# Narrow attention products on TensorE: taken in pairs or when overdue, instead of one by one in the order of their due times

## The chip, the cores and the metric

The kernel runs on one core of one Trainium2 chip. The metric is the device time of one execution in microseconds (us); three executions of each kernel are timed and their median is compared. One further execution is taken by the hardware profiler, and all rows of the profile come from that one.

## What is computed

A windowed attention is followed by two two-layer perceptrons, all in float32:

```python
B, H, S, D = 4, 8, 576, 64              # 2304 tokens, d_model 512, d_ff 2048
rel = pos[:, None] - pos[None, :]
mask = (0 <= rel) & (rel < 32)                          # heads 0 to 3
mask = (0 <= rel) & (rel < 128) & (rel % 4 == 0)        # heads 4 to 7
x = softmax(where(mask, q @ k.T / 8, -1e9)) @ v         # 2304 x 512
x = elu(x @ w1_in) @ w1_out
h = x @ w2_in
out = (h * clip(h + 3, 0, 6) / 6) @ w2_out
```

## The kernel before

**Precision.** Each float32 operand of a wide product is split into a high and a low part, and a product is the sum of three passes (high by high, high by low, low by high). The attention's products are single passes.

**Phase 1** (until about 467 us in the profile) is attention and the first perceptron. The tokens go in five blocks of 384, 512, 512, 512 and 384 columns. Each block goes through 16 slices of d_ff (`tile1`). For each slice, `g1` makes 12 products into PSUM tile `h` (L646), ScalarE and VectorE form the ELU and its split `ghl`, and `g2` makes 12 products into the four tiles `yp` (L702). In the first block the weights are also unpacked and split on VectorE, ScalarE and GpSimd (`convert`, `weights1`; tiles `raw` and `w`).

**Attention** goes in 18 units of 128 tokens (`unit`). Units 0 to 2 feed block 0, 3 to 6 block 1, 7 to 10 block 2, 11 to 14 block 3 and 15 to 17 block 4. The units of a block are spread over the work of the block before. A unit has three narrow products on TensorE, each written as one job:

- `scores` (L486, tile `ps`): 32 products of 64 columns; needs the loaded `q` and `k`, a PSUM bank, and a buffer `s`.
- `turn` (L536, tile `pp`): 4 transposes of 128 columns; needs the softmax of its unit. That is `low` and `top` on VectorE (L493, L502), eight `expos` on ScalarE (L521), `norm` (L527, L528) and `scale` (L531).
- `pv` (L560, tile `po`): 32 products of 64 columns; needs the two copies `turned` of `pp` into `pt`, and `v`. After it, `x_hi` and `x_lo` (L567, tile `xl`) write the block's input.

From unit 3 on, these three share the two PSUM banks of tag `a`. `q`, `k` and `v` have one buffer each, so that the next unit's `q` and `k` are loaded behind this unit's `scores`, and its `v` behind this unit's `pv` (L441, on the DMA queue of SyncE).

**The order of the work** is fixed when the program is written, by a planner (`Plan.run`). Each job has a due time `key`, a cost for each engine that it may run on, the jobs that it needs, and the buffers that it takes. For each engine the planner walks the ready jobs in order of `key`. It takes the first, unless a later one can start over 0.05 us sooner. So an engine never waits while a ready job is left, and a job early by its key fills a hole. The engines then run their queues in exactly this order. Costs and keys are the planner's own estimates.

The due times of units follow from the block starts `TB` (30.0, 107.1, 204.7, 302.3 and 397.2 by the planner's costs):

```python
unit(A1[b] // UN + u, TB[b - 1] + CFG["ATT0"] + u * (TB[b] - TB[b - 1]) * 0.93 / n, 0)
```

With `ATT0` = 3 this gives 33.0, 50.9, 68.9 and 86.8 for units 3 to 6; 110.1, 132.8, 155.5 and 178.2 for units 7 to 10; 207.7, 230.4, 253.1 and 275.7 for units 11 to 14; and 305.3, 334.7 and 364.1 for units 15 to 17. `scores` has the unit's key, `turn` 0.5 more and `pv` 0.7 more.

**Phase 2** is the second perceptron: L900 (tile `hq`) and L989 (tile `m`). The change touches none of its jobs.

Of the kernel before, what the change touches and what calls it, by code (L numbers as in the profile page):

```python
# [40 lines left out]
CFG = dict(  # L41
    T0=30.0, AT=2.6,
    AHEAD=6,
    LEAD=10.0,
    LAG=12.0,
    PREP0=40.0,
    PREP1=-25.0,
    ATT0=3.0,
    LO="P",
    ELU="A",  # L50
    BUFS=dict(g=11, e=2, y=3, ghl=3, q=1, k=1, v=1, pt=1),
    WARM=46.0,
    FROM=1.6,
    FULL=3, MPE=3, KM=5.0,
    VL=3.0,
    S2=5,
# [38 lines left out]
class Plan:  # L95
# [6 lines left out]
    def job(self, key, fn, opts, need=(), dma=0.0, takes=()):  # L102
        j = Job(key, fn, opts, need, dma)
        for ring, users in takes:
            users.append(j)
            j.takes.append((ring, users))
        self.jobs.append(j)
        return j

    def run(self):  # L110
        free = dict.fromkeys("TDAPS", 0.0)
        queue = 0.0
        pool = []
        ready = {e: [] for e in free}
        left = {}

        def enter(j):
            j.ready = max((n.end + lag + (0.25 if n.eng == "T" else 0.1) for n, lag in j.need), default=0.0)
            for e in j.opts:
                ready[e].append(j)  # L120
                ready[e].sort(key=lambda x: x.key)

        for j in self.jobs:
            left[j] = len(j.need)
            for n, _ in j.need:
                n.after.append(j)
        for j in self.jobs:
            if not left[j]:
                enter(j)
        todo = len(self.jobs)  # L130
        while todo:
            best = None
            for e, t0 in free.items():
                pick = None
                for n, j in enumerate(ready[e]):
                    if n >= 60 and pick:
                        break
                    t = max(t0, j.ready)
                    if pick and t > pick[0] - 0.05:
                        continue  # L140
                    for ring, _ in j.takes:
                        r = ring.ready(sum(x is ring for x, _ in j.takes))
                        t = 1e9 if r is None else max(t, r + 0.1)
                    if t >= 1e9 or pick and t > pick[0] - 0.05:
                        continue

                    if any(
                        max(free[o], t) + d < t + j.opts[e] + (CFG["BIAS"] if e == "D" and o == "A" else -0.02)
                        for o, d in j.opts.items() if o != e
                    ):  # L150
                        continue
                    pick = (t, j)
                if pick and (best is None or pick[0] < best[0]):
                    best = (*pick, e)
            assert best, [(e, [(x.key, x.fn) for x in r[:5]]) for e, r in ready.items()]
            t, j, e = best
            d = j.opts[e]
            if e == "T" and t < CFG["WARM"]:
                self.fill(free[e], t)
            for o in j.opts:  # L160
                ready[o].remove(j)
            for ring, users in j.takes:
                ring.take(users)
            j.eng = e
            if e == "D" and getattr(j, "sbuf", True):

                end, w = t, d
                for a, b in pool[-8:]:
                    if b > end:
                        g = max(a - end, 0.0)  # L170
                        if w <= g:
                            break
                        w -= g
                        end += g
                        z = min((b - end) * 0.42, w)
                        w -= z
                        end += z / 0.42
                d = end + w - t
            if e == "P":
                pool.append((t, t + d))  # L180
            free[e] = t + d + (0.0 if e == "T" else 0.02)
            j.end = t + d
            if j.dma:
                queue = max(queue, t + d + 1.4) + j.dma
                j.end = queue + 0.7
            j.fn(e)
            todo -= 1
            for a in j.after:
                left[a] -= 1
                if not left[a]:  # L190
                    enter(a)
# [3 lines left out]
def tile_window_attention_two_mlps(  # L195
# [228 lines left out]
    U1 = A1[1] // UN  # L424

    def unit(u, key, step):
        b = next(b for b in range(NB1) if A1[b + 1] > u * UN)
        t0 = u * UN - A1[b]
# [35 lines left out]
        while sum(w for _, w, _ in runs) < NB:  # L464
            n = sum(w for _, w, _ in runs)
            runs.append((n, next(w for w in range(NB - n, 0, -1) if len(set(masks[n:n + w])) == 1), masks[n]))

        full = u < CFG["FULL"]
        pe_masks = u < CFG["MPE"]
# [103 lines left out]
        n = NB * KW  # L573
        take1 = [(RINGS[tags[0]], bu[0])]
        if pe_masks:
            j0 = job(key - CFG["KM"], masked, {"T": 0.25}, [setup if full else setups], 0, take1)
            bu[0].append(j0)
        j1 = job(
            key, scores, {"T": 0.071 * 2 * NB}, [ld["q"], ld["k"], j0 if pe_masks else setups],
            0, [*([] if pe_masks else take1), (RINGS["s"], su), (RINGS["st"], stu)],  # L580
        )
# [18 lines left out]
        else:  # L600
# [8 lines left out]
        j6 = job(  # L609
            key + 0.5, turn, {"T": 0.12 * NB / 2}, [j5, zeros[u % len(pts)]], 0,  # L610
            [(RINGS[tags[1]], bu[1]), (RINGS[f"p{u % len(pts)}"], pu)],
        )
# [5 lines left out]
        j8 = job(key + 0.7, pv, {"T": 0.066 * 2 * NB}, [*j7, ld["v"]], 0, [(RINGS[tags[2]], bu[2])])  # L618
# [17 lines left out]
            x_users[b][z].extend([j9, j10])  # L636
        x_done.setdefault(b, []).append(j10)
        att_users.extend([j8, j10])


    PASSES = ((0, 0), (0, 1), (1, 0))
# [492 lines left out]
    def fill(t0, t1):  # L1134

        n = int((t1 - max(t0, CFG["FROM"]) - 0.35) / (0.44 if not t0 else 0.24))
        r = RINGS["h"].ready(1)
# [8 lines left out]
    with tc.manual_schedule():  # L1146
# [3 lines left out]
        for u in range(U1):  # L1150
            unit(u, CFG["ATT0"] + CFG["K0"] + u * CFG["KS"], 0)
# [3 lines left out]
        for b in range(1, NB1):  # L1155
            n = W1[b] // UN
            for u in range(n):
                unit(A1[b] // UN + u, TB[b - 1] + CFG["ATT0"] + u * (TB[b] - TB[b - 1]) * 0.93 / n, 0)
# [82 lines left out]
def program(inputs):  # L1241
    import numpy as _np
    import concourse.bacc as _bacc
    import concourse.tile as _tile
    from concourse import mybir as _mybir

    nc = _bacc.Bacc("TRN2", target_bir_lowering=False, num_devices=1, dynamic_dma_scratch_size=1024)
    arrays, args = {}, []
    for name, a in layout(**inputs).items():
        arrays[f"in_{name}_dram"] = a  # L1250
        args.append(nc.dram_tensor(f"in_{name}_dram", a.shape, _mybir.dt.from_np(a.dtype), kind="ExternalInput").ap())
    for i, (shape, dtype) in enumerate(_OUTS):
        dt = _mybir.dt.from_np(_np.dtype(dtype))
        args.append(nc.dram_tensor(f"out_{i}_dram", shape, dt, kind="ExternalOutput").ap())
    with _tile.TileContext(nc) as tc:
        tile_window_attention_two_mlps(tc, *args)
    return nc, arrays
# [8 lines left out]
```

## Time and profile before

| | before |
|---|---|
| median of 3 executions | 864.72 us (862.34 to 866.33) |
| the profiled execution | 864.24 us |
| its span, first to last instruction | 862.5 us |
| TensorE busy | 843.7 us, 98% of the span |
| VectorE, ScalarE, GpSimd busy | 64%, 47%, 14% |
| mean granted TensorE clock | 0.998 |

Units and their products are numbered in the order in which they appear in the trace. PE is TensorE, PEld its weight loads, DVE VectorE, ACT ScalarE, POOL GpSimd, SP SyncE and SPq its DMA queue.

### The profile page before, as it was taken

The page shows a single profiled execution, that of the slowest core. Times are in us where ns is not written, and L with a number is a line of the kernel's source. Part 1 is how long each engine was busy: PE and PEld are TensorE (multiplying, and loading weights), DVE is VectorE, ACT ScalarE, POOL GpSimd, SP SyncE. Part 2 cuts the span into 40 slices and gives each one's busy share as a digit, 9 for nine tenths or more (in the row PEclk, how much of TensorE's full clock was granted, in tenths as well). Part 3 has the DMA queues.
Part 4 walks back from the last instruction along what each step waited for, and adds up shares of the span by engine and source line. Part 5 has one row for each costly group of instructions (what it writes and reads, how often), then busy time and mean ns, then how long its engine had stood idle before and what let it go on. Part 6 is the DMA issues. An engine that isn't in the chain of part 4 may idle for free.

```text
span 862.5 us, 15275 instructions
## 1 busy us (share of the span) xinstructions
PE 843.7 (98%) x5692; PEld 751.1 (87%) x5692; DVE 551.5 (64%) x1156; ACT 403.5 (47%) x999; POOL 123.6 (14%) x137
## 2 busy tenths in 40 slices
PE   8899999999999999999999999999999999999996
PEld 7799988888888888888999888899999999999995
DVE  4999996766878783333343546756575657565673
ACT  3878865666747663242332434333343333333341
POOL 3565431222223300000000000100010010000000
PEclk9999999999999999999999999999999999999999
DMA  9958436877678870300764866887787878789785
GB/s 364 384 208 320 169 136 237 284 269 243 236 263 287 290 270 26 134 1 10 230 207 121 296 243 225 299 274 267 269 292 248 271 273 280 254 278 336 271 265 187
DMA packets 71273, 205.27 MB, mean 238 GB/s; under 512 B 7456, under 2 KB 25888, under 8 KB 71200
## 3 DMA queue, kind: packets, MB, share of 16 engines
q1 hardware_dynamic: 71200, 204.31, 68.4%
q8 instruction: 45, 0.74, 0.3%
q14 instruction: 28, 0.23, 0.1%
HBM read 171.77 MB, written 32.51 MB: 237 GB/s over the span
## 4 chain that ended last, share of the span: by engine, by line
PE 88%; DVE 5%; DMA 4%; ACT 2%; issue 1%; POOL 0%; SPq 0%; DVEq 0%; ACTq 0%; POOLq 0%
PE hq L900 23%; PE yp L702 20%; PE h L646 20%; PE m L989 19%; PE po L560 2%; DMA y<-x2d 2%; PE ps L486 2%; DMA wx<-w2do 1%; DVE raw L306 1%; PE pp L536 1%; DVE raw L303 1%; DVE o L1067 1%; DMA raw<-in_w_in_dram 1%; DVE w L250 1%; ACT pt L250 1%
## 5 line engine op out<-in xcount | busy, mean ns | idle before, releaser
L702 PE MATMUL yp<-ghl,w 128*128 128x512 f32 (+1 forms) x960 | 212.9, 370 | 0.0
L900 PE MATMUL hq<-x,w 128*128 128x512 f32 (+1 forms) x960 | 211.9, 370 | 0.0
L646 PE MATMUL h<-xh,w 128*128 128x512 f32 (+1 forms) x640 | 198.3, 371 | 1.9 <-DVE e L680 1.9
L702 PEld LDWEIGHTS yp<-ghl,w 128*128 128x128 f32 x960 | 173.7, 188 | 23.1
L900 PEld LDWEIGHTS hq<-x,w 128*128 128x128 f32 x960 | 164.5, 189 | 26.5
L646 PEld LDWEIGHTS h<-xh,w 128*128 128x128 f32 x640 | 118.7, 188 | 19.1 <-DVE e L680 3.5
L646 PE MATMUL h<-xl,w 128*128 128x512 f32 (+1 forms) x320 | 117.8, 368 | 0.2 <-DVE xl L567 0.2
L253 DVE TENSOR_TENSOR gz<-gf,gz 128x640 fp32r<-128x640 f32 x72 | 59.2, 823 | 81.4 <-ACT gz L250 81.4
L919 ACT ACTIVATE g<-hq 128x256 f32<-128x256 f32 x144 | 50.7, 383 | 117.3 <-PE hq L900 83.2
L250 ACT CAST gz<-gf 128x640 fp32r<-128x640 f32 x72 | 52.4, 727 | 103.2 <-PE m L989 89.0
L680 DVE SCALAR_TENSOR_TENSOR e<-e,h 128x512 f32<-128x512 f32 (+1 forms) x80 | 50.3, 628 | 76.4 <-ACT e L669 76.1
L666 ACT ACTIVATE e<-h 128x512 f32<-128x512 f32 (+1 forms) x80 | 44.3, 553 | 111.7 <-PE h L646 109.5
L989 PE MATMUL m<-w,gz 128*128 128x256 f32 x648 | 95.3, 283 | 0.0
L924 DVE SCALAR_TENSOR_TENSOR g<-g,hq 128x256 f32<-128x256 f32 x144 | 56.9, 417 | 57.2 <-ACT g L919 53.6
L989 PEld LDWEIGHTS m<-w,gz 128*128 128x128 f32 x648 | 87.4, 191 | 2.3
L646 PEld LDWEIGHTS h<-xl,w 128*128 128x128 f32 x320 | 60.1, 188 | 7.7 <-DVE xl L567 0.4
L989 PE MATMUL m<-wx,gz 128*128 128x256 f32 x432 | 63.6, 283 | 0.0
L253 POOL TENSOR_TENSOR x<-y,x 128x256 fp32r<-128x256 f32 x17 | 13.5, 812 | 328.3 <-ACT x L250 271.9
L989 PEld LDWEIGHTS m<-wx,gz 128*128 128x128 f32 x432 | 57.0, 192 | 0.0
L253 DVE TENSOR_TENSOR ghl<-e,ghl 128x512 fp32r<-128x512 f32 (+1 forms) x77 | 55.6, 722 | 2.3 <-ACT ghl L250 0.2
L306 DVE SCALAR_TENSOR_TENSOR raw<-raw 128x512 int32<-128x512 int32 x64 | 52.5, 828 | 2.3 <-ACT raw L295 0.8
L253 POOL TENSOR_TENSOR w<-raw,w 128x512 fp32r<-128x512 f32 x32 | 46.9, 1475 | 41.9 <-ACT w L250 24.6
(78 smaller groups left out, 959.6 us busy)
## 6 DMA issues: line engine op xcount, KB each, us to landing
wx<-w2do SPq DMA_DIRECT2D x72, 768.0 KB, 4.3
w<-w2di SPq DMA_DIRECT2D x80, 512.0 KB, 5.2
raw<-in_w_in_dram SPq DMA_DIRECT2D x32, 512.0 KB, 5.9
raw<-in_w_out_dram SPq DMA_DIRECT2D x32, 512.0 KB, 6.5
w2do<-stg SPq DMA_DIRECT2D x56, 256.0 KB, 2.3
q<-in_q_dram SPq DMA_DIRECT2D x18, 512.0 KB, 3.8
v<-in_v_dram SPq DMA_DIRECT2D x18, 512.0 KB, 4.0
w2di<-stg SPq DMA_DIRECT2D x32, 256.0 KB, 3.8
```

The lines of the kernel that those rows point to most:

```text
L250: (nc.scalar.copy if e == "A" else nc.vector.tensor_copy)(out=out, in_=in_)
L253: ENG[e].tensor_tensor(out=out, in0=in0, in1=in1, op=ALU.subtract)
L306: nc.vector.scalar_tensor_tensor(out=hi(), in0=hi(), scalar=3, in1=lo(), op0=ALU.logical_shift_left, op1=ALU.bitwise_or)
L486: nc.tensor.matmul(pe[c * KW:(c + 1) * KW, n, :], t["q"][:, c, n, :], kk[:, c], start=not pe_masks, stop=not pe_masks or n == NB - 1)
L646: nc.tensor.matmul(h, w[:, a, c * P:(c + 1) * P], x[b][:, c, :], start=(c == 0 and s == 0), stop=(c == KD - 1 and s == 2),)
L666: nc.scalar.activation(out=r["e"], in_=r["h"], func=AF.Relu, scale=-1.0)
L680: nc.vector.scalar_tensor_tensor(out=r["e"], in0=r["e"], scalar=-1.0, in1=r["h"], op0=ALU.add, op1=ALU.max)
L702: nc.tensor.matmul(ys[b, n], w[:, a, n * P:(n + 1) * P], g[:, c, :], start=(i == 0 and s == 0), stop=(i == KF - 1 and s == 2),)
L900: nc.tensor.matmul(r["h"], w[:, a, d * P:(d + 1) * P], x2[c, d][:, z, :], start=(d == 0 and s == 0), stop=(d == KD - 1 and s == 2),)
L919: nc.scalar.activation(out=g_t[b, j][:, k], in_=r["h"][:, h * N2:(h + 1) * N2], func=AF.Relu, bias=3.0)
L924: nc.vector.scalar_tensor_tensor(out=g_t[b, j][:, k], in0=g_t[b, j][:, k], scalar=6.0, in1=r["h"][:, h * N2:(h + 1) * N2], op0=ALU.min, op ...
L989: nc.tensor.matmul(ms[k], g, w[:, c, :], start=(j == 0 and z == 0 and s == 0), stop=(j == KP - 1 and z == len(PRODS[n]) - 1 and s == 2),)
```

## The change

For units 3 to 17 the three jobs `scores`, `turn` and `pv` (`j1`, `j6`, `j8`) are marked `short`. When the planner chooses for TensorE at its time `t0`, it looks at the short jobs whose needs are met by then (`j.ready <= t0`; whether a buffer is free is not asked). There are three cases:

1. If the job that TensorE took last was short and another short one is ready, that one goes ahead of everything else.
2. Otherwise, if exactly one short job is ready and `t0` is below its key plus `WAIT` (6 us), it is left out of the choice, also where TensorE would have nothing else to do.
3. Otherwise the order is that of before.

```diff
+    WAIT=6.0,
...
         todo = len(self.jobs)
+        last = False
         while todo:
             best = None
             for e, t0 in free.items():
                 pick = None
-                for n, j in enumerate(ready[e]):
+
+                short = [j for j in ready[e] if getattr(j, "short", False) and j.ready <= t0] if e == "T" else []
+                if last and short:
+                    order = short + [j for j in ready[e] if j not in short]
+                elif len(short) == 1 and t0 < short[0].key + CFG["WAIT"]:
+                    order = [j for j in ready[e] if j not in short]
+                else:
+                    order = ready[e]
+                for n, j in enumerate(order):
                     if n >= 60 and pick:
                         break
...
+            if e == "T":
+                last = getattr(j, "short", False)
...
+        if u >= U1:
+            for x in (j1, j6, j8):
+                x.short = True
```

## Rows read from the trace of the kernel before

**Rows 1.** Busy time by stretch: length, busy us (instructions) by engine, granted clock, DMA share, GB/s.
```profile
core 0: us, PE busy (x) PEld busy (x) DVE busy (x) ACT busy (x) POOL busy (x), PEclk, DMA share, GB/s
...
25.00:40.00 15.00, 12.45 (x128) 11.45 (x125) 14.57 (x26) 12.41 (x36) 9.90 (x7) 1.00 0.94 369
40.00:60.00 20.00, 18.87 (x186) 17.88 (x185) 19.70 (x29) 15.19 (x41) 10.28 (x8) 1.00 0.60 226
60.00:80.00 20.00, 19.46 (x163) 18.55 (x162) 19.96 (x31) 16.71 (x43) 10.52 (x7) 1.00 0.85 311
80.00:104.00 24.00, 23.82 (x212) 22.59 (x212) 23.65 (x38) 20.73 (x51) 12.90 (x9) 1.00 0.55 200
...
120.00:416.00 296.00, 296.00 (x1839) 244.09 (x1838) 187.59 (x352) 159.57 (x399) 52.87 (x57) 1.00 0.56 194
```

**Rows 2.** Chain of work that ended last, 153 to 172 us: start, us, what.
```profile
154.28 1.08 PE ps L486 x32
155.37 2.94 PE yp L702 x12
158.31 2.72 PE h L646 x12
161.03 2.72 PE yp L702 x12
163.75 0.44 PE pp L536 x4
164.19 2.77 PE h L646 x12
166.96 1.08 PE po L560 x32
168.05 2.94 PE yp L702 x12
```

**Rows 3.** The same chain where two narrow products touch, units 11, 12 and 15, 16.
```profile
218.93 0.44 PE pp L536 x4
219.37 1.08 PE ps L486 x32
220.45 2.94 PE h L646 x12
...
318.39 1.08 PE ps L486 x32
319.47 0.58 PE pp L536 x4
320.06 2.77 PE yp L702 x12
```

**Rows 4.** SP's DMA queue behind unit 9's scores: start, us, engine, line, what.
```profile
155.41 0.33 SPq L441 DMA_DIRECT2D q<-in_q_dram  x1
```

**Rows 5.** DMA issues by kind: count, KB each, median us from issue to landing.
```profile
q<-in_q_dram SPq DMA_DIRECT2D x18, 512.0 KB, 3.8
```

**Rows 6.** TensorE's timeline: scores of unit 3, unit 4; unit 5, then the rest of unit 4.
```profile
25.05 1.10 PE L486 MATMUL ps<-k,q 128*64 128x64 f32 x32
...
35.70 1.15 PE L486 MATMUL ps<-k,q 128*64 128x64 f32 x32
38.87 0.63 PE L536 MATMUL pp<-ident,s 128*128 128x128 f32 x4 [2.03 <-ACT w L250]
...
53.22 1.15 PE L486 MATMUL ps<-k,q 128*64 128x64 f32 x32
54.30 0.66 PE L536 MATMUL pp<-ident,s 128*128 128x128 f32 x4
...
58.20 1.15 PE L560 MATMUL po<-pt,v 128*64 128x64 f32 x32 [1.13 <-DVE s L493]
```

**Rows 7.** TensorE's timeline: scores of unit 6; units 5, 7; units 6, 8, 6.
```profile
63.67 1.15 PE L486 MATMUL ps<-k,q 128*64 128x64 f32 x32
...
78.19 0.60 PE L536 MATMUL pp<-ident,s 128*128 128x128 f32 x4
78.72 1.15 PE L486 MATMUL ps<-k,q 128*64 128x64 f32 x32
...
95.92 0.63 PE L536 MATMUL pp<-ident,s 128*128 128x128 f32 x4
96.48 1.15 PE L486 MATMUL ps<-k,q 128*64 128x64 f32 x32
97.81 1.15 PE L560 MATMUL po<-pt,v 128*64 128x64 f32 x32 [0.18 <-ACT pt L250]
```

**Rows 8.** VectorE's timeline: last inputs (`xl`) of block 1 and of block 3.
```profile
101.30 0.68 DVE L567 TENSOR_TENSOR xl<-po,xh 128x512 fp32r<-128x512 f32 x1
...
296.71 0.69 DVE L567 TENSOR_TENSOR xl<-po,xh 128x512 fp32r<-128x512 f32 x1
```

**Rows 9.** TensorE's timeline: block 1's first product, block 0's left-over products, block 3's first.
```profile
103.20 0.39 PE L646 MATMUL h<-xh,w 128*128 128x512 f32 x1
...
108.07 4.33 PE L702 MATMUL yp<-ghl,w 128*128 128x384 f32 x24
...
306.04 0.39 PE L646 MATMUL h<-xh,w 128*128 128x512 f32 x1
```

## The prediction

> **What bounds the kernel now.** The busy times by stretch come first, as they show where TensorE's order can matter [rows 1]. From 120 to 416 us TensorE is busy for all of its 296.00 us, at a granted clock of 1.00. There only its own work counts: whatever a narrow product costs it is paid in full, and nothing is waited for. From 25 to 104 us it is different. VectorE is busy 14.57 + 19.70 + 19.96 + 23.65 = 77.88 of 79 us, while TensorE has 12.45 + 18.87 + 19.46 + 23.82 = 74.60. In this stretch VectorE, with the unpacking of weights, sets the pace, and TensorE has 4.4 us of holes. The change adds and removes no instruction. It can act in three ways: by what it costs TensorE to go between wide and narrow products, by the holes, and by the lateness of a block's input.
>
> The chain of waits prices the first one, where TensorE is the bound [rows 2]. A wide group of 12 takes 2.72 us on the chain, but 2.94 behind a `scores` or a `pv`, and 2.77 behind a `turn`. So a `scores` or a `pv` alone costs 1.08 + 0.22 = 1.30 us, and a `turn` alone 0.44 + 0.05 = 0.49.
>
> **What the rule does, followed by hand.** Here I need which jobs are ready together. The due times are in the section on the kernel. They hold well where TensorE is the bound: unit 9's `scores` (due 155.5) starts at 154.28 on the chain [rows 2].
>
> A unit's `scores` frees `q` and `k`. Unit 9's started at 154.28, and the next `q` is issued at 155.41 [rows 2, 4]. A load lands 3.8 us after its issue [rows 5], so the next unit's `scores` is ready about 5 us behind the one before. A unit's `turn` comes later, as its softmax stands between: 9.5 us behind for unit 9 (163.75 - 154.28) [rows 2], 13.8 for unit 3 (38.87 - 25.05) [rows 6]. So when `turn` of unit u is ready, `scores` of unit u+1 already waits. Two short jobs are ready, the old order holds, `turn` has the smaller key and goes first, and `scores` of u+1 is pulled behind it.
>
> - Unit 3's `scores` ran at 25.05 [rows 6], 8 us ahead of its key 33.0. Now it is alone and held to about 33 + 6 = 39.
> - Its `turn` is ready at 49 to 53 and carries unit 4's `scores` with it (before: 35.70). In the same way units 5 and 6 come at about 64 and 78, against 53.22 and 63.67 [rows 6, 7].
> - From there on `scores` runs with the `turn` of the unit before, so a unit's softmax is done before its key is due, and `turn` u with `scores` u+1 goes at about the key of u.
> - `pv` came 3.2 us behind its `turn` (166.96 - 163.75) [rows 2], as two copies lie between; the `scores` carried along takes 1.08. So `pv` isn't ready then. A wide group follows, then `pv` by itself. The next `scores`, 5 us behind the last, isn't there to join it.
>
> So 14 pairs form (`turn` of units 3 to 16 with the next `scores`). Before, five pairs already touch: units 4 and 5 [rows 6], 5 and 7, 6 and 8 [rows 7], 11 and 12, 15 and 16 [rows 3]. Nine are new.
>
> **What a pair is worth.** The pair of units 11 and 12 takes 0.44 + 1.08, and the wide group behind it 2.94 [rows 3]. That is 1.74 over a plain group, against 0.49 + 1.30 = 1.79 apart: 0.05 us saved. The other way round (15 and 16) it takes 1.08 + 0.58 + 0.05 = 1.71, so 0.08 saved [rows 3]. Nine new pairs at 0.05 give 0.45 us. Two products of 64 columns side by side, `scores` and `pv`, don't stand in a stretch where TensorE is the bound. There one boundary would go, so between 0 and 0.22 us; I take none, as the rule as followed makes none. The upper bound, nine pairs at 0.22, is 2.0 us.
>
> The Trainium skill (TensorE: Matmul & The Clock Gate, Part 2, steps 1 and 5) says that a weight load is pulled ahead of running matmuls when it doesn't conflict with them, and that the drain of one matmul overlaps the fill of the next. By that a boundary would cost nothing, joining would save nothing, and the sum would be 864.7. The rows disagree by 0.22 and 0.05 us [rows 2].
>
> **The stretch from 25 to 104 us.** Three things change there, and I take their sum as nothing, because VectorE sets the pace (77.88 of 79 us) and does the same work.
> - `scores` of units 3 to 6 leave the places at 25.05, 35.70, 53.22 and 63.67 [rows 6, 7]. If all four sat in holes and now stand where TensorE is the bound, that costs 4 x 1.30 = 5.2 us.
> - Against it, the work behind unit 3's `scores` no longer competes with the weights between 25 and 39. The hole of 2.03 us at 38.87, a wait on ScalarE's `w` [rows 6], can shrink.
> - At 58.20 `pv` of unit 4 waited 1.13 us on VectorE's `s`, that is on `low` of unit 5, whose `scores` had taken a PSUM bank just ahead of `turn` 4 [rows 6]. With `turn` first, `pv` comes into the bank of its own `turn`, for whose copies it waits anyway. That wait should go.
>
> All holes together are 4.4 us [rows 1], which bounds the gain.
>
> **A block's input.** Block 1's last `xl` ends at 101.98, and its first product starts at 103.20: 1.2 us to spare, and block 0's products left over (4.33 us) could go ahead [rows 8, 9]. By the steps above `scores` of unit 6 comes at about 78. Its `turn` ran at 95.92, some 32 us after its `scores` [rows 7], since `low` of unit 6 has its own key, 86.9, on a full VectorE; this stays. For block 3 the margin is 306.04 - 297.40 = 8.6 us [rows 8, 9], and the units now run earlier: `turn` 14 at about 276, and `xl` at about 283. So this costs nothing; what covers it is the margin, and beyond it each microsecond would count in full.
>
> **The sum.** 864.24 of the profiled execution less 0.45 is 863.8. The median of the three runs is 0.5 above that execution, so 864.72 - 0.45 = 864.3; with the wait at 58.20 left out of account I say 864.2. A difference under 0.5% (4.3 us) can't be told from no change: the three runs alone spread over 4.0 us.
>
> **The rivals.**
> 1. *Held products leave holes; slower.* The second case leaves a lone job out also where TensorE has nothing else. The pairs at 219.37 and 318.39 ran 11 and 16 us ahead of their keys (230.4 and 334.7) [rows 3], so before they filled holes. It decides if the weights don't come earlier by what unit 3 gives free. Then the four `scores` between 25 and 64 us are paid again at 1.30 each, and the time is about 864.7 - 0.5 + 5.2 = 869.4. Half of it would give 866.8. For it: TensorE's holes in the stretch. Against it: VectorE's 77.88 of 79 us. Chance 0.17; in 0.13 over 0.5% slower.
> 2. *Pairs are worth a whole boundary, and the holes close; faster.* Nine pairs at 0.22 (2.0 us), with the holes of 2.03 and 1.13 us gone, give 864.7 - 5.2 = 859.5. Against it: the pair of units 11 and 12 saved 0.05. Chance 0.14; in 0.09 over 0.5% faster.
> 3. *The pairs don't form.* `scores` alone waits for its key plus 6 and goes by itself, and `turn` and `pv` are overdue whenever they are ready. Then nothing is saved. Block 1's input comes last: unit 6's `scores` at 86.8 + 6 = 92.8, `turn` 9.5 later, `pv` 3.2 after that, and the `xl` that ended 4.2 behind its `pv` (101.98 - 97.81) [rows 7, 8], so 109.7, 6.5 us after the first product that needs it, of which block 0's products left over cover 4.3. That gives 864.7 + 2.2 = 866.9 at most, 864.7 if more wide work is found. For it: unit 9's three products each stood alone [rows 2]. Against it: the load lands 5 us behind. Chance 0.09.
>
> My forecast has 0.60. By cases: faster by over 0.5% 0.10, within 0.5% 0.76, slower 0.14. The range, 860.5 to 868.0, leaves out the full price of rival 1 and the far end of rival 2.
>
> **What the changed profile would show.** `ps` right behind `pp` for some 14 units, in the order `turn`, `scores`; `po` alone; unit 3's `scores` near 39; `xl` of unit 14 near 283 instead of 296.71. TensorE stays at 100% from 120 to 416 us, and the chain has pairs of 0.44 + 1.08 with 2.94 behind. I'm wrong in mechanism if `po` touches a `ps`, or if `scores` stands alone at its key plus 6. I'm wrong in size if the busy share of TensorE between 25 and 104 us moves by more than 2 us, or if block 1 starts later than 105.

## The result: slower by 0.7%, outside the range

| | before | changed |
|---|---|---|
| median of 9 executions | 863.05 us (860.71 to 866.33) | 868.91 us (866.95 to 870.74) |
| profiled execution, its span | 864.24, 862.5 | 867.27, 865.6 |
| mean granted TensorE clock in it | 0.998 | 0.996 |

The ratio is 1.0069 (95% interval 1.0053 to 1.0086). The same program timed twice more, each time beside the kernel before, gave 1.0043 and 1.0062. I had said 864.2, at most 868.0. The profiled execution of the changed kernel is 1.6 us under its median and that of before 1.2 us over (863.05), so the two profiles show 3 of the 5.9 us; two more profiles of the changed kernel help.

The busy times by stretch of the changed kernel, with the columns of [rows 1]:

```profile
core 0: us, PE busy (x) PEld busy (x) DVE busy (x) ACT busy (x) POOL busy (x), PEclk, DMA share, GB/s
...
38.90:42.30 3.40, 3.40 (x38) 2.96 (x37) 3.40 (x5) 3.31 (x7) 2.31 (x2) 0.50 0.22 86
...
25.00:120.00 95.00, 87.86 (x734) 81.89 (x735) 89.89 (x138) 75.26 (x198) 49.49 (x34) 0.98 0.63 234
120.00:416.00 296.00, 294.66 (x1856) 242.85 (x1855) 188.01 (x350) 160.63 (x409) 55.96 (x61) 1.00 0.57 196
416.00:440.00 24.00, 24.00 (x140) 23.93 (x139) 9.47 (x20) 8.80 (x20) 0.00 (x0) 1.00 0.74 232
```

and of the kernel before, from 120 to 416 us in [rows 1]:

```profile
25.00:120.00 95.00, 89.85 (x790) 84.36 (x787) 93.59 (x148) 76.53 (x213) 48.82 (x34) 1.00 0.67 246
416.00:440.00 24.00, 22.93 (x131) 22.30 (x130) 8.79 (x19) 7.11 (x16) 0.00 (x0) 1.00 0.85 270
```

Four things differ. From 25 to 120 us TensorE is idle for 7.14 of 95 us; in the kernel before it is 5.15 (89.85 busy), and VectorE has fallen from 93.59 to 89.89. From 120 to 416 TensorE lacks 1.34 us where it lacked none. From 38.9 to 42.3 us the granted clock is 0.50, that is 1.2 of 2.4 GHz, where it was 1.00. And 416 to 440 us gives 1.07 us back: it is full, and was busy for 22.93.

TensorE's timeline shows what the rule did (start, us, engine, line, operation, idle before it). The change moves the lines: `scores` is now L498, `turn` L548, `pv` L572, the products of `g1` L661 and of `g2` L717.

```profile
38.58 0.81 PE L548 MATMUL pp<-ident,s 128*128 128x128 f32 x4 [3.09 <-ACT w L262]
39.31 1.98 PE L498 MATMUL ps<-k,q 128*64 128x64 f32 x32
...
75.24 0.60 PE L548 MATMUL pp<-ident,s 128*128 128x128 f32 x4
75.77 1.15 PE L498 MATMUL ps<-k,q 128*64 128x64 f32 x32
...
98.04 0.63 PE L548 MATMUL pp<-ident,s 128*128 128x128 f32 x4
98.60 1.15 PE L498 MATMUL ps<-k,q 128*64 128x64 f32 x32
...
115.97 0.63 PE L548 MATMUL pp<-ident,s 128*128 128x128 f32 x4 [1.44 <-DVE s L543]
116.53 1.15 PE L498 MATMUL ps<-k,q 128*64 128x64 f32 x32
```

These are `turn` 3 with `scores` 4 (was 35.70), 5 with 6 (was 63.67), 6 with 7 (was 78.72) and 7 with 8 (was 96.48) [rows 6, 7]. `scores` of units 7 and 8 come 20 us later. The hole ahead of `turn` 3 grew from 2.03 to 3.09 us, and `turn` 7 has a new wait of 1.44 us (1.50 and 2.01 in the other two profiles).

The chain that ended last shows a pair that I hadn't expected, `pv` with `scores`:

```profile
228.85 0.68 PE h L661 x3
229.54 1.08 PE po L572 x32
230.62 0.93 PE ps L498 x32
231.55 2.95 PE yp L717 x12
```

It costs 1.08 + 0.93 + (2.95 - 2.72) = 2.24 us, against 2 x 1.30 apart [rows 2]: 0.36 saved, where `turn` with `scores` saves 0.05.

### The profile page after: what moved, and what is told of

Same layout as the page of the kernel before. It is cut to its first block, busy times and chain, and to the rows that moved or that the text cites. A ratio compares the mean times of both kernels' runs of the same rounds, so it can differ in the third digit from the quotient of the medians.

```text
span 865.6 us, 15285 instructions
## 1 busy us (share of the span) xinstructions
PE 845.5 (98%) x5692; PEld 753.4 (87%) x5692; DVE 550.7 (64%) x1150; ACT 405.9 (47%) x1001; POOL 127.5 (15%) x141
## 4 chain that ended last, share of the span: by engine, by line
PE 84%; DVE 6%; DMA 6%; issue 1%; POOL 1%; ACT 1%; SPq 1%; DVEq 0%; ACTq 0%; POOLq 0%
PE hq L915 23%; PE m L1004 20%; PE yp L717 19%; PE h L661 18%; DMA raw<-in_w_in_dram 2%; DMA v<-in_v_dram 1%; PE ps L498 1%; DMA k<-in_k_dram 1%; PE po L572 1%; DVE raw L318 1%; DVE raw L315 1%; PE pp L548 1%; POOL w L265 1%; DMA wx<-w2do 1%; DVE ghl L265 1%
## 5 line engine op out<-in xcount | busy, mean ns | idle before, releaser
L717 PE MATMUL yp<-ghl,w 128*128 128x512 f32 (+1 forms) x960 | 213.6, 370 | 1.9 <-DVE ghl L265 1.3
L661 PE MATMUL h<-xh,w 128*128 128x512 f32 (+1 forms) x640 | 198.2, 371 | 1.3 <-DVE e L695 0.7
L717 PEld LDWEIGHTS yp<-ghl,w 128*128 128x128 f32 x960 | 173.8, 188 | 26.8 <-DVE ghl L265 2.8
L661 PEld LDWEIGHTS h<-xh,w 128*128 128x128 f32 x640 | 119.0, 188 | 18.3 <-POOL w L265 0.9
L661 PE MATMUL h<-xl,w 128*128 128x512 f32 (+1 forms) x320 | 117.8, 368 | 0.0
L661 PEld LDWEIGHTS h<-xl,w 128*128 128x128 f32 x320 | 60.3, 188 | 7.3
L318 DVE SCALAR_TENSOR_TENSOR raw<-raw 128x512 int32<-128x512 int32 x64 | 55.3, 869 | 4.4 <-ACT raw L307 2.8
```

Source lines behind the costliest of these rows:

```text
L318: nc.vector.scalar_tensor_tensor(out=hi(), in0=hi(), scalar=3, in1=lo(), op0=ALU.logical_shift_left, op1=ALU.bitwise_or)
L661: nc.tensor.matmul(h, w[:, a, c * P:(c + 1) * P], x[b][:, c, :], start=(c == 0 and s == 0), stop=(c == KD - 1 and s == 2),)
L717: nc.tensor.matmul(ys[b, n], w[:, a, n * P:(n + 1) * P], g[:, c, :], start=(i == 0 and s == 0), stop=(i == KF - 1 and s == 2),)
```

## The experiments

Each run was timed in 5 rounds beside the kernel before. Edits are to the changed kernel unless it says the kernel before. "Idle" is length less busy time of TensorE in the run's own profile; in the kernel before it is 5.15 and 0.00 us. The letters in the expectations: A, the loss comes between 25 and 104 us, by the hole ahead of `turn` 3 and the clock behind it; B, it comes from 120 us on; C, `scores` of 7 and 8 are held out of the stretch that VectorE bounds; D, the new places of units 9 to 17 make VectorE or a DMA queue late; E, the hold of unit 7 alone does it; H, the holds of 7 and 8 together.

| run | median, us | before, us | ratio (95%) | idle 25 to 120 | idle 120 to 416 |
|---|---|---|---|---|---|
| changed, first time | 868.91 | 863.05 | 1.0069 (1.0053 to 1.0086) | 7.14 | 1.34 |
| changed, again | 867.7 | 863.57 | 1.0043 (1.0023 to 1.0062) | 7.30 | 0.79 |
| changed, a third time | 868.73 | 863.27 | 1.0062 (1.0043 to 1.0081) | 7.81 | 1.26 |
| 1 only units 3 to 6 | 862.27 | 862.54 | 0.9997 (0.9985 to 1.001) | 4.88 | 0.00 |
| 2 only from unit 7 | 866.01 | 862.54 | 1.0039 (1.0021 to 1.0057) | 5.09 | 1.05 |
| 3 put last, not left out | 865.02 | 862.54 | 1.002 (1.0007 to 1.0032) | 5.00 | 3.97 |
| 4 hole filled | 866.71 | 862.54 | 1.0043 (1.0029 to 1.0057) | 3.60 | 1.94 |
| 4 again | 868.84 | 863.27 | 1.006 (1.004 to 1.0079) | 4.08 | 3.63 |
| 5 before, hole filled | 865.54 | 863.27 | 1.0025 (1.0011 to 1.0039) | 3.05 | 1.32 |
| 6 only from unit 9 | 863.9 | 863.57 | 1.0008 (0.9993 to 1.0024) | 4.91 | 1.44 |
| 7 `scores` 7, 8 free | 862.46 | 863.57 | 0.9992 (0.9974 to 1.001) | 4.97 | 0.97 |
| 8 `scores` 8 free | 863.92 | 863.34 | 1.0007 (0.9985 to 1.0029) | 6.03 | 0.26 |
| 9 `scores` 4, 7, 8 free | 866.56 | 861.99 | 1.0041 (1.0023 to 1.0058) | 4.87 | 3.96 |
| 10 before, 7 held | 863.92 | 863.34 | 1.001 (0.9994 to 1.0025) | 5.28 | 1.33 |
| 11 before, 7 and 8 held | 865.1 | 861.99 | 1.0025 (1.0006 to 1.0043) | 5.17 | 0.36 |
| 12 7 with holes filled | 862.94 | 863.27 | 1.0004 (0.9987 to 1.0021) | 1.59 | 3.19 |
| 13 `pv` pulls `scores` | 864.4 | 863.57 | 1.0015 (0.9996 to 1.0033) | 5.11 | 4.54 |
| 14 13 with the hold | 870.07 | 863.34 | 1.0078 (1.0051 to 1.0106) | 4.95 | 6.26 |

By the medians, runs 2, 3, 5, 9, 13 and 14 fell outside every forecast made for them (3.5, 2.5, 2.3, 4.6, 0.8 and 6.7 us over the kernel before). So did run 7, 5.2 us under the changed kernel timed with it, and the second timing of the changed kernel (4.1 us over).

**Where it comes from: units 3 to 6, or later ones (1, 2).**

```diff
-        if u >= U1:
+        if U1 <= u < 7:      # run 1;  run 2: if u >= 7:
```

> Only units 3 to 6 are marked short; units 7 to 17 keep the old rule. Theory A (the loss is made between 25 and 104 us: a held scores leaves TensorE's hole before unit 3's turn empty, the clock falls in it, and the work behind it is late): nearly the whole loss stays, 4 to 6 us over the kernel before. Theory B (the loss is made from 120 us on, where TensorE now waits for VectorE's ghl behind weight loads that come late on the DMA queue): within 1.5 us of the kernel before.

> Only units 7 to 17 are marked short; the first part up to unit 6 has the order of before. Theory A: within 2 us of the kernel before, or under it by the 1 to 2 us that the pairs save. Theory B: 4 to 6 us over it.

Run 1 equals the kernel before, to within 0.2%, and A falls. Its profile keeps the hole of 3.1 us ahead of `turn` 3 and the new places of `scores` 4 to 6, and yet:

```profile
25.00:120.00 95.00, 90.12 (x762) 84.90 (x759) 91.50 (x148) 75.92 (x212) 47.96 (x33) 0.98 0.66 243
120.00:416.00 296.00, 296.00 (x1863) 243.88 (x1858) 186.98 (x347) 160.06 (x400) 58.45 (x61) 1.00 0.56 195
```

TensorE is busy 0.27 us more than before from 25 to 120 us, and full after. Units 7 to 17 alone (run 2) cost 0.4%, the larger part.

**The second case itself (3).**

```diff
-                    order = [j for j in ready[e] if j not in short]
+                    order = [j for j in ready[e] if j not in short] + short
```

> A lone short job that isn't due is put last in the choice instead of out of it, so that it may still fill a hole; the pulling ahead stays. Theory A: 0 to 3 us under the kernel before, since scores of unit 4 is back in its hole and the pairs of pv with the next scores save 0.37 us each. Theory B: still 3 us or more over it, as the pulled scores still move the loads.

A lone short job may now go where TensorE would have nothing else. A third to a half of the loss is left. The idle time from 25 to 120 us is back at 5.00, and from 120 us on it is 3.97, three times that of the changed kernel. So one hole went and others came.

**The clock (4, 5, 12, and the changed kernel twice more).**

```diff
+            if u == 3:
+                for _ in range(16):
+                    nc.tensor.matmul(pp[:, 0, :], ident, ident, start=True, stop=True)
```

This puts 16 products that nobody reads ahead of `turn` 3, into the hole; in 4 to the changed kernel, in 5 to the kernel before, in 12 to run 7.

> The changed kernel with 16 more products ahead of unit 3's transposes, written to the place that the transposes then overwrite; they need nothing but the bank, so they run in the hole before unit 3's turn. The hole's work stays missing, but TensorE isn't idle for 3.09 us. Theory A with the clock's share: the granted clock stays at 1.00 there, unit 4's scores takes 1.08 us instead of 1.91, and the time falls by about 1.5 us from the changed kernel, to 4 us over the kernel before. If the clock had no share: no change from the changed kernel (within 0.7 us).

> The changed kernel once more, beside the others: 5 to 7 us over the kernel before in its median, with its profile between 1 and 2 us of clock at the lower level in the stretch from 30 to 60 us.

> The changed kernel with the 16 products in the hole, once more, this time on the same chip as the changed kernel. If the clock has a share: 1 to 2 us under the changed kernel; if not, within 0.7 us of it.

> The changed kernel, for the comparison with the three others: 4 to 6 us over the kernel before.

> The kernel before with the same 16 products in its hole of 2.03 us before unit 3's turn. If the clock falls there in some executions (the mean granted clock of its runs was 0.9976 to 0.998): 0.5 to 1.5 us under it, with a mean granted clock near 0.999. If it doesn't: the same within 0.7 us.

> The changed kernel with scores of units 7 and 8 not marked, and with the 16 products of no use ahead of unit 3's transposes (overwritten by them), so that TensorE isn't idle in the 3.09 us before unit 3's turn. If the clock's fall behind that hole is a loss of its own: 1 to 2.5 us under the kernel before, as the kernel without these products was 1.1 under it. If it costs nothing in the end: 0 to 1 us under.

Filling the hole changed nothing: 868.84 us against 868.73 of the changed kernel timed beside it, and run 12 (1.0004) is no faster than run 7 (0.9992). In the changed kernel the products fit the hole, as run 4's timeline shows:

```profile
35.07 3.73 PE L549 MATMUL pp<-ident 128*128 128x128 f32 x32
38.64 0.60 PE L551 MATMUL pp<-ident,s 128*128 128x128 f32 x4
```

`turn` 3 starts where it did (38.58), its transposes take 0.60 us instead of 0.81, and the granted clock is 1.00 from 36 to 46 us. Over the six executions of "4 again" the mean granted clock is 0.9988, against 0.9957 for the changed kernel beside it. Either the clock's fall costs nothing in the end, or what filling the hole gives back is lost elsewhere: these two profiles idle for 1.94 and 3.63 us from 120 us on, for 0.79 to 1.34 without the products. Which of the two holds isn't shown. In the kernel before the same products don't fit. Run 5's timeline:

```profile
36.98 3.84 PE L537 MATMUL pp<-ident 128*128 128x128 f32 x32
40.66 0.60 PE L539 MATMUL pp<-ident,s 128*128 128x128 f32 x4
```

The 16 products take 3.84 us, and `turn` 3 starts at 40.66 instead of 38.87 [rows 6]. They outlast the hole by 1.8 us, and run 5 is 2.3 us slower. So there this edit isn't a clean test.

The hole of the changed kernel doesn't bring the clock down each time. It is 3.09 or 3.10 us in all three profiles, and behind it the clock was 0.50 in the first (row above). The second profile has, in the same stretch,

```profile
38.90:42.30 3.40, 3.39 (x46) 3.16 (x47) 3.40 (x6) 3.28 (x7) 2.27 (x2) 1.00 0.45 166
```

and the third, 1.3 us later,

```profile
40.20:43.60 3.40, 3.40 (x23) 3.28 (x20) 3.40 (x7) 2.32 (x5) 1.49 (x2) 0.52 0.50 154
```

So the clock fell in the first and the third, and not in the second. Each timed execution also lists its mean granted clock. Over 138 executions of the kernel before (those beside the runs), the time goes from a mean of 861.8 us at 1.000 (21 of them) over 863.4 at 0.997 (46) to 865.2 at 0.995 (9), 0.7 us for each 0.001. The changed kernel's 26 have a mean clock of 0.9965 against 0.9978, so by this about 0.9 of the 5.0 us between the two means go with the clock. At equal clock the rest stands: 867.8 (8 executions) against 863.4 (46) at 0.997, and 869.3 (6) against 865.2 (9) at 0.995. This is a comparison of executions and not an edit that sets the clock. Run 4 is such an edit, and its gain of 0.003 in the mean clock brought no time. So the share of the clock stays open, and most of the loss is there without it.

**Which units (6 to 11).**

```diff
-        if u >= U1:
+        if u >= 9:                                                      # run 6
...
-            for x in (j1, j6, j8):
+            for x in (j6, j8) if u in (7, 8) else (j1, j6, j8):         # run 7
+            for x in (j6, j8) if u == 8 else (j1, j6, j8):              # run 8
+            for x in (j6, j8) if u in (4, 7, 8) else (j1, j6, j8):      # run 9
```

and to the kernel before's order, with the rule's code in place:

```diff
+        if u in (6, 7):          # run 11; run 10: u == 6
+            j6.short = True
+        if u in (7, 8):          # run 11; run 10: u == 7
+            j1.short = True
```

> Only units 9 to 17 are marked, so that scores of units 7 and 8 keep their places at 78.72 and 96.48 us, where VectorE sets the pace. Theory C (what costs from unit 7 on is that these two scores are held out of that stretch and then paid at 1.21 us each where TensorE is the bound, 2.4 us): within 1 us of the kernel before. Theory D (the new places of units 9 to 17 cost, as VectorE and the DMA queue come late behind them): 2 to 4 us over it, as with units 7 to 17.

> The changed kernel, but scores of units 7 and 8 are not marked. In the order written, units 3 to 6 are as in the changed kernel and these two scores run at about 80 and 97 again. Theory C: 2 to 3.5 us under the changed kernel. Theory D: within 1 us of the changed kernel.

> The changed kernel, with scores of unit 8 not marked; scores of unit 7 stays held to about 97 us. Theory E: still 2.5 us or more over the kernel before, so that the gain of freeing units 7 and 8 together is unit 7's. Rival G (it is unit 8's scores that counts): within 1.5 us of the kernel before.

> The kernel before with one thing alone from the change: scores of unit 7 is held until turn of unit 6 is ready, about 97 us instead of 78.72; its q and k are then freed late, so scores of unit 8 comes at about 110 instead of 96.48. All else keeps its rule. Theory E (this one hold makes most of the loss: TensorE's places between 80 and 104 us stay empty, unit 7's turn comes late behind a full VectorE, and a scores or two is paid at 1.21 us from 104 us on): 2 to 4 us over the kernel before. Rival F (the loss needs the new order of all units): within 1 us of it.

> The kernel before, with scores of units 7 and 8 both held, each until the turn of the unit before it. In the order written they come at about 97 and 113 us (before: 78.72 and 96.48). Theory H (holding both is what costs: the place ahead of unit 7's turn stays empty, TensorE waits there for 1.4 to 2 us, and one more scores is paid at 1.21 us where TensorE is the bound): 2.5 us or more over the kernel before. Rival J (the holding costs little by itself; the loss needs the new order from unit 9 on): within 1 us of it.

> A try at a better kernel: the changed kernel with scores of units 4, 7 and 8 not marked, so that unit 4's scores is back in the hole before unit 3's turn and no idle stretch of 3.09 us stands there. If that hole and the clock's falls behind it cost 1 to 2 us: 1 to 2 us under the kernel before. If the new order takes it back by waits of TensorE from 120 us on: 0 to 3 us over it.

Runs 2 and 6 differ in the marks of units 7 and 8 alone: with them 0.4% is lost, without them 0.1%, less than its interval. With `scores` of 7 and 8 free the whole loss is gone (0.9992), and with 8 alone free nearly so (1.0007), as C says. E falls: holding 7 alone costs 0.1%, less than its interval. The wait of 1.44 us ahead of `turn` 7 is absent where `scores` 8 is free. Here is run 8's timeline, in which `scores` 8 and `turn` 7 go without a wait:

```profile
111.27 1.15 PE L498 MATMUL ps<-k,q 128*64 128x64 f32 x32
...
118.05 0.60 PE L548 MATMUL pp<-ident,s 128*128 128x128 f32 x4
```

But runs 7 and 8 free more than two jobs: the order behind them changes too. `pv` stands next to a following `scores` 4 times in the changed kernel, 7 times in run 7 and 8 times in run 8, and `turn` next to a following `scores` 10, 6 and 5 times. At 0.36 and 0.05 us each this is about 1 us of the gain.

Holding 7 and 8 in the kernel before's order costs 0.25% of the 0.43 to 0.69%. By the medians (3.1 us) H's time came and J's did not. H's mechanism didn't come, for in run 11 `turn` 7 waits for nothing:

```profile
112.76 0.60 PE L548 MATMUL pp<-ident,s 128*128 128x128 f32 x4
```

And C isn't the whole of it: run 9 frees 4 as well as 7 and 8, and has 0.41% of loss back, with 3.96 us idle from 120 us on. The loss isn't that of a unit. It is that of an order as a whole.

One rival is untested in all of these runs. With each new order the planner also chooses anew which engine does a job of the weights or of the ELU. The lines of busy time on the two pages, before and changed:

```profile
PE 843.7 (98%) x5692; PEld 751.1 (87%) x5692; DVE 551.5 (64%) x1156; ACT 403.5 (47%) x999; POOL 123.6 (14%) x137
PE 845.5 (98%) x5692; PEld 753.4 (87%) x5692; DVE 550.7 (64%) x1150; ACT 405.9 (47%) x1001; POOL 127.5 (15%) x141
```

TensorE has the same instructions, the other three don't. VectorE has 120 instructions that write `raw` instead of 128, and ScalarE 86 instead of 78; for `w` it is 17 instead of 13 and 15 instead of 19, and GpSimd writes `stg` 34 times instead of 29. No run holds these choices fixed, so what the places of the narrow products cost by themselves isn't separated from it.

**The cheap pair alone (13, 14).** `pv` with `scores` saves most, so 13 drops the second case and lets only `pv` pull a `scores`, from unit 9 on; 14 does the same and keeps the second case for `scores`.

```diff
-                elif len(short) == 1 and t0 < short[0].key + CFG["WAIT"]:          # run 13 alone
-                    order = [j for j in ready[e] if j not in short]                # run 13 alone
...
-                last = getattr(j, "short", False)
+                last = getattr(j, "lead", False)
...
+        if u >= 9:
+            j1.short = True
+            j8.lead = True
```

> From unit 9 on the next scores is pulled only behind a pv, and nothing is held. pv with scores behind it takes 2.15 us against 2.42 apart, so some six pairs could save 1.6 us. Theory C: 0 to 1.6 us under the kernel before. Theory D: 1 to 3 us over it, by waits of TensorE at the pulled scores and at the wide groups behind them.

> A try at a better kernel: from unit 9 on only scores is held, and pulled only behind a pv; everything up to unit 8 is as before. Eight pairs of pv and scores at 0.27 us each would save 2.2 us; two neighbours of before that saved 0.08 or nothing are lost. If nothing else moves: 1 to 2 us under the kernel before. If new waits of TensorE take it back, as in the kernel that pulled without holding: 0 to 2 us over it.

Neither won. In 14 the hold makes TensorE wait for 6.26 us from 120 us on, the most of all runs, and the waits are spread (what waits, for whom, us in total, times, longest):

```profile
PE yp L717 <- ACT y L262: 3.1, 2, 1.8
PE h L661 <- DVE e L695: 1.1, 3, 0.5
PE po L572 <- DVE pt L262: 1.0, 2, 0.8
```

Idle time alone doesn't rank the runs. From 120 us on, runs 3 and 13 idle for 3.97 and 4.54 us and cost 0.2 and 0.15%; runs 2 and 11 idle for 1.05 and 0.36 and cost 0.39 and 0.25%. Each idle time is that of a single execution.

## Why the prediction was wrong, step by step

**The stretch from 25 to 104 us: the step that failed.** "I take their sum as nothing, because VectorE sets the pace" held for units 3 to 6, as run 1 shows. The stretch to 120 us then lost 2.0 to 2.7 us of TensorE's time all the same (7.14 to 7.81 idle for 5.15), since I stopped at unit 6. With the same products done, the changed kernel is 3.0 to 5.1 us behind at 120 us (the balance, below). The rule moved `scores` 7 and 8 by 20 us, and with them VectorE's `low` and `top`. Nor did VectorE do "the same work", as the engines were chosen anew. It was then no longer full: 89.89 us for 93.59. That by itself doesn't decide, for runs 7 and 8 have 90.81 and 90.84 and lose nothing. VectorE's waits from 25 to 120 us in the changed kernel (in the kernel before only 0.8 us in all):

```profile
DVE raw L315 <- DMA raw<-in_w_out_dram: 1.9, 1, 1.9
DVE xl L579 <- ACT xh L262: 1.6, 3, 1.0
```

The chain of work shows the first one on its way to `turn` 7:

```profile
109.70 1.32 POOL w L265
111.03 0.02 issue
111.05 3.22 DMA raw<-in_w_out_dram
...
114.36 0.43 DVE raw L315
...
115.14 0.70 DVE s L543
115.84 0.14 issue
115.97 0.63 PE pp L548 x4
```

GpSimd's `w` frees a buffer for `raw`, the weights load into it, VectorE's queue stands still for them (1.92 us), and unit 7's `norm` and `scale` are behind in that queue. `turn` 7 is at the head of TensorE's queue and pulls `scores` 8 behind it. In the kernel before VectorE has other work at this place and waits for nothing. I had priced the products moved, and not the queues behind them. That this wait is a part of the loss agrees with run 8 and isn't shown alone; its 1.4 to 2.0 us is not the whole, and run 11 loses time without it.

**"Nothing is waited for" from 120 to 416 us** was read from the old order and taken over to the new one. It was 1.34 us, where I had said that TensorE stays at 100%. One microsecond of it is at 155 us. On the chain, a pair frees `q` and `k` at 141.9, SyncE's queue issues the two loads, then stores, then a weight load that lands at 151.5, and VectorE and TensorE follow in order:

```profile
140.38 0.44 PE pp L548 x4
140.82 1.10 PE ps L498 x32
...
141.94 0.35 SPq L453
...
143.81 7.70 DMA raw<-in_w_in_dram
...
151.60 0.13 DVE raw L315
...
154.10 1.34 DVE ghl L265
```

That `scores` is unit 9's, at 154.28 before [rows 2]: the pull brings jobs forward too. Of the orders run here, only those of the kernel before and of run 1 wait for nothing from 120 to 416 us; the others lose 0.3 to 6.3 us there. That the early loads cause it is read from the chain and not tried.

**The pairs: right in number, mis-sized.** 14 formed. 10 are `turn` with `scores`, at 0.05 us. The other 4 are `pv` with `scores`, which I said don't form ("`pv` by itself"), at 0.36. Less the five neighbours of before (0.3 us by my own prices) this is 0.5 + 1.4 - 0.3 = 1.6 us, where I had 0.45, and my bound of 0.22 for a pair was too low. So the gain that the rule aims at is there, and more than it is lost. A `po` that touches a `ps` was my own sign of a wrong mechanism, and it came four times. The prices of a lone product stood: 1.30 and 0.49. The Trainium skill (TensorE: Matmul & The Clock Gate, Part 2, steps 1 and 5) says that a weight load is pulled ahead of running matmuls when it doesn't conflict with them, and that the drain of one matmul overlaps the fill of the next. I had read this as a free boundary; four pairs that save 0.36 us each speak against that more clearly than [rows 2] did.

**The smaller steps.** `scores` 3 was not held, though I had said so. It ran at 25.45, behind a wait of 0.78 us for its `k`; that it wasn't ready in the plan either, and so not left out, is my reading and not shown. The hole at 38.87 didn't shrink but grew by 1.06 us. The wait of 1.13 us ahead of `pv` 4 went, as forecast. Block 1 started at 105.34 (103.20 before), past the 105 that I had named as wrong in size; its last `xl` had ended at 104.09, so the delay is that of the work ahead. `xl` of unit 14 came early, at 290.87 for 296.71 (I said 283), and nothing waited for it.

**The rivals.** The side was that of rival 1, held products that leave holes, to which I gave 0.17. Its time (869.4) is near by luck: it named the `scores` between 25 and 64 us, at 1.30 each, and moving those cost nothing (run 1). The held products that go with a loss are those of units 7 and 8 (runs 2, 6 and 11), which it left out.

**The balance.** Ahead of block 4's first product every order has done the same work. On the chain it starts so in the kernel before, in the three profiles of the changed kernel, and in run 8:

```profile
399.76 2.10 PE h L646 x12
...
404.90 2.10 PE h L661 x12
...
402.73 2.10 PE h L661 x12
...
405.78 2.10 PE h L661 x12
...
399.71 2.10 PE h L661 x12
```

The changed kernel is 5.1, 3.0 and 6.0 us behind there, and run 8 is not. At 120 us it is already 4.2, 3.0 and 5.1 us behind, and run 8 2.2, if the products done by then are counted at the price that each has alone (0.227 and 0.174 us for a wide product of 512 and 384 columns, 1.30 and 0.49 for the narrow jobs). So most of the loss is made by then, in the stretch that I had put at nothing and the 16 us behind it, and run 8 makes its part good afterwards, with eight pairs of `pv` and `scores`.

In the first profile 1.7 of the 4.2 us is slow clock (`turn` 3, `scores` 4 and one `h` at 0.81 + 1.91 + 2.77 for 0.44 + 1.08 + 2.29 on the chain), 2.0 idle, and 0.5 I haven't found. From 120 us on it falls back by 1.2 us at 155, 0.7 at 196, and 0.5 in two `yp` groups of 2.91 and 3.01 instead of 2.72 us behind 300, and gains 1.6 by the pairs. That gives 5.0 of the 5.1 us. The end of phase 1 gives 1.8 back, and phase 2 differs by up to 3 us between profiles (run 1 starts it with the kernel before and ends 3.1 us ahead). The three medians lie 4.1 to 5.9 us over those of before, so this accounts for the size only to some 1 to 2 us.

What stays open is why holding 7 and 8 costs 0.25% (run 11), with idle times of 5.17 and 0.36 us, hardly more than before; and what the new choice of engines costs. No version beat the kernel before by more than its interval: the lowest ratios are 0.9992 and 0.9997.

## What to carry to other kernels

In an order written by a planner, pairing cheap jobs isn't a local edit. Price the pair (0.05 to 0.36 us here), but then follow each moved job to its consumers, to the engines that the planner then picks, and to what its freed buffers let load, through every in-order queue, and past the last unit that the argument names. A stretch with no waits (296.00 of 296.00 us) is a property of that one order, and a new order should be charged some microseconds of waits until its trace shows otherwise. "Another engine sets the pace" covers a delay only while that engine's own inputs stay on time.

## What was not expected of the hardware

- Two narrow groups of 64 columns side by side (`pv`, `scores`) take 2.24 us, 0.36 less than apart; 128-column transposes beside a 64-column group save 0.05.
- A product of 128x128 in float32 shows as two records of 0.12 us: 16 took 3.84 us in 32 records.
- The granted clock behind a hole of one and the same length isn't fixed. Behind 3.1 us idle it fell to half in two executions of one program and stayed at 1.00 in a third. Behind 2.0 us it was 1.00 in the kernel before and 0.50 in run 2's profile, here by stretch:

```profile
39.80:43.20 3.40, 3.40 (x18) 2.96 (x18) 3.21 (x7) 1.99 (x4) 0.31 (x1) 0.50 1.02 408
```

Part of the spread of 5 us that one kernel shows goes with this, 0.7 us of time for each 0.001 of the mean granted clock. That the clock makes it isn't shown.
